# An FFT mixing layer before two MoE layers on one core: where the sums over thirds of x are made, in which step a weight decode takes its Abs, and by which order background sums are taken

## The chip, the cores and the metric

The kernel runs on one core of a Trainium2 chip. The metric is the time of one execution on the device in microseconds (us), taken as the median of several runs. The core has five engines with instruction queues of their own: TensorE (PE in the rows, PEld its weight loads), VectorE (DVE), ScalarE (ACT), GpSimd (POOL) and SyncE (SP, which here only issues transfers). Each queue is worked off in order; an instruction that waits holds everything behind it on its engine.

## The reference, cut to what matters

```python
def reference(x, w_r, w_i, b_r, b_i, moe.., moe2..):      # x: [4, 3072, 256] float32
    X = rfft(x, axis=1)                                    # per batch, along 3072
    Yr = Xr @ w_r - Xi @ w_i + b_r;  Yi = Xr @ w_i + Xi @ w_r + b_i
    Y = soft_threshold(Yr, 0.01) + 1j * soft_threshold(Yi, 0.01)
    y = irfft(Y, n=3072, axis=1)
    h = y @ w_in;  g = h * tanh(softplus(h));  z = g @ w_out      # moe, d_ff 2048
    # moe2: a token mix with the token before, relu(xk @ w_k)**2 @ w_v, times sigmoid(xr @ w_r)
```

The weights of the two MoE layers come as 64-bit floats and are decoded to 32 bits on the chip.

## The kernel before, in words

The program has two parts. `part1` (up to 361.54 us in the profiled execution) does the Fourier mixing of all four batches, one batch after the other; `part2` does the MoE layers and is laid out by a planner of its own (`Plan`). The change touches `part1` alone.

A sequence of 3072 is seen as 24 x 128. The forward transform takes radix sums over the 24 lines of x (`f1_ops`, VectorE, 128x1024 to 128x256 at a time) and then, for each of 12 residues, a product over the 128 (`emit_F`). A batch of x lies in SBUF as a tile `a` of 32 lines: three thirds of eight lines each (0 to 7, 8 to 15, 16 to 23, `load_third`), and eight lines (24 to 31) of room. There are two such tiles, in turn for the batches. The radix sums of a batch begin with the difference of the second and last third and with the sum of all three, called S here; then S - 3 times the first third, by `stt(..., -3.0, ...)` at L309, called the -3 combination here. S is made by transfers: after the difference, `sum_x` (L365) issues two accumulating transfers from GpSimd's queue, which add the second and the first third of x from DRAM onto lines 16 to 23. Batch 0 makes its sums by `f1_fast` and is not touched.

`part1` then runs a loop of 48 steps u (`NU`, twelve per batch, t = u % 12). TensorE's work of step u is the forward product F(u+1) (`emit_F`, or `emit_F3` with x split in a high and a low plane where u+1 is in `SPLIT_F`), the mixing product M(u) with the weights w_r and w_i (`emit_M`) and the inverse product I(u-1) (`emit_I`, split in planes where u-1 is in `SPLIT_I`). Behind them ScalarE and VectorE do: `post_F` (xh on ScalarE, xl on VectorE, both operands of M), `post_M` and `post_M2` (the threshold: yb on ScalarE, then on VectorE), for a split I the planes zh (ScalarE) and zl (VectorE), `post_I` (bs on ScalarE, then a store from SP to b_dr; bs has three buffers), and `preload` (the bias into a PSUM bank). The planes of the inverse matrices (imhi, imlo) come over GpSimd's queue into a ring of 12 slots (`load_stream`), a slot's next load being issued in the step that frees it.

Work off this path goes into the gaps of VectorE by `Background`: a queue `q` of the forward sums, each with a due step, and a list `f3` of the inverse radix sums of batch 0 (`f3_ops`, tile g, two jobs put in at steps 14 and 20, load of g first, stores to y_dr among the sums). `until(t)` issues such work while a clock that the program keeps by itself (70 ns + 1.04 ns an element) stays below t, always taking `q` first; `flush(due)` issues all of `q` that has come due; `drain` issues all that is left at step 42.

At steps 7 to 47 the weights of the first MoE layer are decoded by `Weights`: eight groups of w_in and four pieces of w_out. In step `first` of a piece ScalarE makes the sign (two instructions), VectorE builds the 32-bit word (two), and ScalarE takes Abs of it; in the step after, VectorE combines Abs with the sign and, for a group, makes four sums; later (`late`) ScalarE makes the high parts and VectorE, a step after that, the low parts. Groups 0 to 3 start at steps 11, 12, 23 and 24, groups 4 to 7 at 37 to 40, the pieces of w_out at 41 to 44; the high parts of the eight groups are at 35 to 42.

`new_a` (L694 on) loads all three thirds of batch b+2 from SP in step 10 of batch b, into a tile that it takes anew.

## Time and profile before

| | |
|---|---|
| median of 3 runs | 1910.03 us (1907.85 to 1910.5) |
| profiled execution | 1910.78 us, its span 1908.9 us |
| granted TensorE clock, mean | 0.989 |
| TensorE busy | 1856.1 us, 97% of the span |
| VectorE busy | 1427.9 us, 75% |
| ScalarE busy | 1220.8 us, 64% |
| GpSimd busy | 65.3 us, 3% |
| accumulating and other transfers on GpSimd's queue | 27.79 MB, 6.3% of 16 transfer engines |

The span is the stretch from the first to the last instruction. Times inside it are counted from its start. Loop step 6 begins at 54.65 us, step 12 at 106.27, step 24 at 185.73, step 32 at 245.62, step 40 at 299.03, step 46 at 348.73 (each the start of that step's F product); the second part begins at 361.54.

### The profile page before, as it was taken

To read this page: it belongs to the slowest core of one execution; us is meant where nothing else is said; L and a number is where in the kernel's file an instruction comes from. 1 tells how busy PE (TensorE), PEld (TensorE's weight loads), DVE (VectorE), ACT (ScalarE), POOL (GpSimd) and SP (SyncE) were. 2 spreads that over 40 slices of the span, in tenths; PEclk is the share of its full clock that TensorE was granted. 3 is DMA by queue.
4 is the path that set the end of the run, shared out by engine and by line. 5 is a ranking of instruction groups with operands and counts; after the bars stand their busy time and mean duration, and the time that the engine had idled before them with its cause. 6 is when DMAs were issued, how large, how long until landed. Compare 5 with 4: busy or idle time off the path is not lost.

```text
span 1908.9 us, 27281 instructions
## 1 busy us (share of the span) xinstructions
PE 1856.1 (97%) x9814; PEld 1602.4 (84%) x9814; DVE 1427.9 (75%) x2548; ACT 1220.8 (64%) x2194; POOL 65.3 (3%) x111
## 2 busy tenths in 40 slices
PE   9789897999999999999999999999999999999999
PEld 7678786788888888888888888888899999999998
DVE  8669797689888977778877777675676666667654
ACT  3245465667576575766757566574877777777775
POOL 1121221000000000000000000000000000000000
PEclk9899998999999999999999999999999999999999
DMA  9697979555566563646455554544422222222211
GB/s 314 133 246 209 229 201 289 195 174 167 152 202 190 159 190 117 190 132 192 153 174 160 161 188 140 163 152 130 139 83 67 67 67 67 67 67 69 70 51 34
DMA packets 192598, 283.87 MB, mean 149 GB/s; under 512 B 17104, under 2 KB 106960, under 8 KB 192208
## 3 DMA queue, kind: packets, MB, share of 16 engines
q1 hardware_dynamic: 173248, 253.29, 42.1%
q0 software_dynamic: 18144, 27.79, 6.3%
q8 instruction: 78, 1.28, 0.3%
q10 hardware_dynamic: 1072, 1.05, 0.2%
q14 instruction: 56, 0.46, 0.1%
HBM read 205.52 MB, written 76.55 MB: 148 GB/s over the span
## 4 chain that ended last, share of the span: by engine, by line
PE 88%; DMA 4%; DVE 4%; ACT 2%; SPq 1%; issue 1%; POOL 0%; ACTq 0%; DVEq 0%; POOLq 0%
PE a L218 27%; PE x L218 15%; PE v L218 14%; PE c L218 10%; PE z L218 5%; PE d L218 5%; PE zps L218 3%; PE yps L218 3%; DMA a<-in_x_dram 3%; PE xps L218 2%; PE bps L218 2%; DMA y_dr<-g 1%; DMA b_dr<-bs 1%; DVE g L209 1%; SPq L392 0%
## 5 line engine op out<-in xcount | busy, mean ns | idle before, releaser
L209 DVE TENSOR_TENSOR l<-k,h 128x512 fp32r<-128x512 f32 x576 | 391.6, 688 | 309.8 <-ACT h L215 155.0
L218 PE MATMUL a<-h,wo 128*128 128x512 f32 x1536 | 520.2, 389 | 0.0
L218 PEld LDWEIGHTS a<-h,wo 128*128 128x128 f32 x1536 | 288.3, 188 | 59.8
L218 PE MATMUL a<-l,wo 128*128 128x512 f32 x768 | 298.8, 389 | 0.0
L218 PE MATMUL v<-wv,h 128*128 128x256 f32 x1536 | 274.3, 278 | 0.0
L218 PEld LDWEIGHTS v<-wv,h 128*128 128x128 f32 x1536 | 244.3, 188 | 13.6
L218 PE MATMUL x<-yc,wr 128*128 128x512 f32 x864 | 243.5, 390 | 1.0 <-ACT c L215 1.0
L215 ACT ACTIVATE k<-c 128x512 f32<-128x512 f32 x288 | 172.7, 600 | 105.5 <-PE c L218 93.6
L215 ACT ACTIVATE c<-x 128x512 f32<-128x512 f32 x288 | 169.5, 589 | 92.4 <-PE x L218 77.9
L215 ACT ACTIVATE k<-k 128x512 f32<-128x512 f32 x288 | 178.2, 632 | 64.8 <-DVE k L209 62.3
L218 PE MATMUL v<-wv,l 128*128 128x256 f32 x768 | 213.0, 277 | 0.0
L218 PEld LDWEIGHTS x<-yc,wr 128*128 128x128 f32 x864 | 161.8, 188 | 36.2 <-ACT c L215 2.3
L215 ACT ACTIVATE d<-x 128x512 f32<-128x512 f32 x144 | 84.5, 587 | 147.9 <-PE x L218 146.6
L218 PEld LDWEIGHTS a<-l,wo 128*128 128x128 f32 x768 | 144.1, 188 | 30.3
L218 PE MATMUL c<-yc,wr 128*128 128x512 f32 x576 | 161.9, 389 | 0.0
L218 PEld LDWEIGHTS v<-wv,l 128*128 128x128 f32 x768 | 144.4, 188 | 0.0
L215 ACT ACTIVATE h<-k 128x512 fp32r<-128x512 f32 x192 | 118.7, 629 | 27.8 <-DVE k L212 25.8
L209 DVE TENSOR_TENSOR k<-d,zs 128x512 f32<-128x512 f32 x144 | 98.8, 686 | 44.7 <-PE d L218 44.6
L218 PEld LDWEIGHTS c<-yc,wr 128*128 128x128 f32 x576 | 108.1, 188 | 22.6
L209 DVE TENSOR_TENSOR yc<-src,yc 128x512 fp32r<-128x512 f32 x168 | 112.0, 686 | 14.4 <-ACT yc L215 14.0
L218 PE MATMUL x<-yc,wk 128*128 128x512 f32 x432 | 122.5, 392 | 0.0
L209 DVE TENSOR_TENSOR g<-g 128x128 f32<-128x128 f32 (+3 forms) x264 | 111.1, 443 | 0.9
(121 smaller groups left out, 2924.4 us busy)
## 6 DMA issues: line engine op xcount, KB each, us to landing
wr<-h_dr SPq DMA_DIRECT2D x288, 256.0 KB, 2.7
b_dr<-bs SPq DMA_DIRECT2D x48, 256.0 KB, 3.7
src<-y_dr SPq DMA_DIRECT2D x24, 512.0 KB, 4.3
wr<-h_dr SPq DMA_DIRECT2D x96, 128.0 KB, 2.1
xk_dr<-tm SPq DMA_DIRECT2D x48, 256.0 KB, 3.1
xr_dr<-tm SPq DMA_DIRECT2D x48, 256.0 KB, 3.1
src<-xk_dr SPq DMA_DIRECT2D x24, 512.0 KB, 4.3
xr<-xr_dr SPq DMA_DIRECT2D x24, 512.0 KB, 3.8
```

Of the source, the lines that this page charges most:

```text
L209: V.tensor_tensor(out=o, in0=a, in1=b, op=op)
L215: S.activation(out=o, in_=i, func=f, **kw)
L218: T.matmul(out=o, lhsT=l, rhs=r, start=start, stop=stop, **kw)
```

## The change

For batches 2 and 3 S is no longer made in lines 16 to 23 after the difference. In step 6 of the batch that uses the same tile before, SP loads the first third of x into lines 24 to 31 and the last third into 16 to 23, and `end_sum` adds the second and the last third onto 24 to 31 by accumulating transfers from GpSimd's queue, in halves; in step 10 SP loads the second and the first third. The tile is kept and not taken anew. For batch 1 S is made by VectorE, in four additions of 128x1024. The radix sums behind S use other lines in consequence, and a batch's forward sums all enter the queue in one step: step 4 for batch 1, step 0 of the batch ahead (12 and 24) for the others.

`until` takes inverse sums first while the next forward sum is due more than four steps ahead (`EARLY`).

Abs of a piece is issued in the step after its word, behind the high parts of that step on ScalarE, and the combination with the sign stands at the end of VectorE's work in that step. The high parts are issued right behind `post_M2`, and from step 35 on bs is copied behind xh. Steps 36 to 38 multiply F unsplit: `SPLIT_F` loses 37, 38 and 39.

```diff
@@ -35,14 +35,15 @@
 
 
 
-F1_AT = ((4, 6), (0, 3), (0, 3))
+F1_AT = ((4, 4), (0, 0), (0, 0))
+EARLY = 4
 START = (18600, 20500)
 SLACK = (2000, 3200)
 
 SUMS_AT = (11, 12, 23, 24)
 LOWS_AT = 35
 SPLIT_I = (*range(6, 10), *range(12, 22), *range(24, 34), *range(36, 47))
-SPLIT_F = (37, 38, 39, 44, 45, 46)
+SPLIT_F = (44, 45, 46)
 FIRST = tuple(u + 1 for u in SPLIT_I)
 F3_PART1 = {(1, 2): [(0, 0)], (1, 8): [(0, 1)]}
 ORD = [0, 1, 2, 3, 4, 6, 8, 10, 5, 7, 9, 11]
@@ -50,8 +51,8 @@
 F3_ORDER = [0, 1, 2, 3, 4, 5, 6, 7, 8, 9, 10, 14, 15, 11, 12, 13, 16, 17, 18, 19, 20, 27, 21, 22,
             23, 24, 25, 26, 30, 31, 28, 32, 29, 33, 34, 35, 41, 42, 36, 43, 37, 38, 44, 45, 39, 40, 46, 47]
 T_H, T_K = 10.22, 11.85
-LINES_G = [4, 5, 6, 7, 12, 13, 14, 15]
-LINES_F = [(20, 21), (22, 23), (18, 19), (16, 17),
+LINES_G = [4, 5, 6, 7, 12, 14, 13, 15]
+LINES_F = [(20, 22), (21, 23), (18, 19), (16, 17),
            (24, 25), (2, 10), (28, 29), (3, 11), (26, 27), (6, 14), (30, 31), (7, 15)]
 
 
@@ -305,18 +306,20 @@
         l1 = lambda l: A[:, l]
         one = lambda n, f: [(n, f)]
         head = [
+            halves(8, lambda i, j: tt(L(24 + i, 24 + j), L(8 + i, 8 + j), L(16 + i, 16 + j), ADD)),
             halves(8, lambda i, j: tt(L(8 + i, 8 + j), L(16 + i, 16 + j), L(8 + i, 8 + j), SUB)),
-            halves(8, lambda i, j: stt(L(i, j), L(i, j), -3.0, L(16 + i, 16 + j), MULT, ADD)),
-            one(4, lambda: tt(L(24, 28), L(16, 20), L(20, 24), ADD)),
-            one(4, lambda: tt(L(28, 32), L(16, 20), L(20, 24), SUB)),
-            one(2, lambda: tt(L(16, 18), L(24, 26), L(26, 28), ADD)),
-            one(2, lambda: tt(L(18, 20), L(24, 26), L(26, 28), SUB)),
-            one(1, lambda: tt(l1(20), l1(16), l1(17), ADD)),
-            one(1, lambda: tt(l1(21), l1(16), l1(17), SUB)),
-            one(1, lambda: tt(l1(16), l1(29), l1(31), SUB)),
-            one(1, lambda: tt(l1(17), l1(29), l1(31), ADD)),
-            one(2, lambda: stt(L(22, 24), L(16, 18), HALF, L(28, 31, 2), MULT, ADD)),
-            one(2, lambda: stt(L(16, 18), L(16, 18), -HALF, L(28, 31, 2), MULT, ADD)),
+            halves(8, lambda i, j: tt(L(24 + i, 24 + j), L(i, j), L(24 + i, 24 + j), ADD)),
+            halves(8, lambda i, j: stt(L(i, j), L(i, j), -3.0, L(24 + i, 24 + j), MULT, ADD)),
+            one(4, lambda: tt(L(16, 20), L(24, 28), L(28, 32), ADD)),
+            one(4, lambda: tt(L(20, 24), L(24, 28), L(28, 32), SUB)),
+            one(2, lambda: tt(L(24, 26), L(16, 18), L(18, 20), ADD)),
+            one(2, lambda: tt(L(18, 20), L(16, 18), L(18, 20), SUB)),
+            one(1, lambda: tt(l1(16), l1(21), l1(23), SUB)),
+            one(1, lambda: tt(l1(17), l1(21), l1(23), ADD)),
+            one(2, lambda: stt(L(21, 24, 2), L(16, 18), HALF, L(20, 23, 2), MULT, ADD)),
+            one(2, lambda: stt(L(16, 18), L(16, 18), -HALF, L(20, 23, 2), MULT, ADD)),
+            one(1, lambda: tt(l1(20), l1(24), l1(25), ADD)),
+            one(1, lambda: tt(l1(22), l1(24), l1(25), SUB)),
         ]
         rows = lambda f: [(4, lambda r=r: f(r)) for r in range(2)]
         tail = [
@@ -362,9 +365,11 @@
             for a in (1, 2, 0):
                 load_third(A, b, a, 8 * a, nc.scalar if b == 0 and a == 2 else nc.sync, lo, up)
 
-    def sum_x(A, b):
-        for a in (1, 0):
-            load_third(A, b, a, 16, nc.gpsimd, accum_op=ADD)
+    def end_sum(A, b):
+        for lo in (0, 4):
+            load_third(A, b, 1, 24, nc.gpsimd, lo, lo + 4, accum_op=ADD)
+        for lo in (0, 4):
+            load_third(A, b, 2, 24, nc.gpsimd, lo, lo + 4, accum_op=ADD)
 
     def f3_ops(b, h):
         st = {}
@@ -466,7 +471,8 @@
         def add(self, ops, due=0):
             self.q.extend((c, e, due) for c, e in ops)
 
-        def step(self):
+        def step(self, u=0):
+            self.u = u
             if self.wait:
                 self.wait -= 1
             if not self.f3 and self.jobs:
@@ -486,7 +492,9 @@
         def until(self, t):
 
             while True:
-                q = self.q or (self.f3 if not self.wait else None)
+                q = self.q
+                if self.f3 and not self.wait and (not q or q[0][2] > self.u + EARLY):
+                    q = self.f3
                 if not q or self.clock + q[0][0] > t:
                     return
                 o = q.pop(0)
@@ -630,13 +638,13 @@
         def put(self, step, make, first, late):
             def load():
                 p = make()
-                for u, k, f in ((first, 0, lambda: p[1]()), (first + 1, 0, lambda: p[2]()), (late + 1, 0, lambda: p[4]()),
-                                (first, 1, lambda: p[0]()), (late, 1, lambda: p[3]()), (first, 2, lambda: p[5]())):
+                for u, k, f in ((first, 0, lambda: p[1]()), (first + 1, 4, lambda: p[2]()), (late + 1, 0, lambda: p[4]()),
+                                (late, 1, lambda: p[3]()), (first + 1, 2, lambda: p[5]()), (first, 2, lambda: p[0]())):
                     self.at.setdefault((u, k), []).append(f)
             self.at.setdefault((step, 3), []).append(load)
 
-        def vec(self, u):
-            return [op for f in self.at.get((u, 0), []) for op in f()]
+        def vec(self, u, k=0):
+            return [op for f in self.at.get((u, k), []) for op in f()]
 
         def sca(self, u, k):
             return [op for f in self.at.get((u, k), []) for op in f()]
@@ -926,14 +934,14 @@
             for u in range(NU):
                 b, t = divmod(u, NT)
                 if b + 1 < NB:
-                    if t == F1_AT[b][0]:
-                        head, tail = f1_ops(As[b + 1])
-                        bg.add(priced(head[:1]) + [(0.0, lambda b=b: sum_x(As[b + 1], b + 1))], NT * (b + 1))
-                    if t == F1_AT[b][1]:
-                        for ops, due in ((head[1:], 0), (tail[:10], 4), (tail[10:], 8)):
-                            bg.add(priced(ops), NT * (b + 1) + due)
+                    for k in range(2):
+                        if t == F1_AT[b][k]:
+                            head, tail = f1_ops(As[b + 1])
+                            early = head[1:2] if b else head[:2]
+                            for ops, due in ((head[2 + (b > 0):], 0), (tail[:10], 4), (tail[10:], 8)) if k else ((early, 0),):
+                                bg.add(priced(ops), NT * (b + 1) + due)
                 bg.jobs += F3_PART1.get((b, t), [])
-                bg.step()
+                bg.step(u)
                 if u == SUMS_AT[0] - 4:
                     wf = src_p.tile([128, 4, 8, 128], F32, tag="src", name="wsrc")
 
@@ -961,9 +969,9 @@
                 if u:
                     bg.until(y_at + (900 if u - 1 in SPLIT_I else SLACK[0]))
                     post_M2(u - 1)
-                    if u in FIRST:
-                        if u >= SUMS_AT[0] - 3:
-                            emit(wq.sca(u, 1))
+                    if u >= SUMS_AT[0] - 3:
+                        emit(wq.sca(u, 1))
+                    if u in FIRST and u < LOWS_AT:
                         post_I(u - 2)
                     y_at = bg.spend(y_at, 602)
                     if u - 1 in SPLIT_I:
@@ -971,21 +979,23 @@
                         bg.until(y_at + 900)
                         split_lo(u - 1)
                         y_at = bg.spend(y_at + 900, 602)
+                if u >= SUMS_AT[0] - 3:
+                    emit(wq.sca(u, 2))
                 if u + 1 < NU:
                     bg.until(pe + 700 + SLACK[1] * (u > 0))
                     post_F(u + 1)
                     x_next = bg.spend(pe + 700, 602)
                 if u >= SUMS_AT[0] - 3:
-                    if u not in FIRST:
-                        emit(wq.sca(u, 1))
                     bg.flush(-1)
-                    emit(wq.sca(u, 2))
+                    for c, e in wq.vec(u, 4):
+                        bg.clock += c
+                        e()
                     emit(wq.load(u))
                 if u + 2 in SPLIT_F:
                     split_x(u + 2, 0)
                     split_x(u + 2, 1)
                     bg.clock += 602
-                if u > 1 and u not in FIRST:
+                if u > 1 and (u not in FIRST or u >= LOWS_AT):
                     post_I(u - 2)
                 emit_M(u, None if u else 1)
                 if u + 2 < NU:
@@ -1002,8 +1012,14 @@
                     load_fwd(u + NT)
                 if u == 1:
                     P.tensor_copy(out=zero[:, 32:33], in_=xt[2][0][:, 0, 0:1].bitcast(F32))
+                if t == NT - 6 and b + 2 < NB:
+                    A = As[b + 2] = As[b]
+                    load_third(A, b + 2, 0, 24, nc.sync)
+                    end_sum(A, b + 2)
+                    load_third(A, b + 2, 2, 16, nc.sync)
                 if t == NT - 2 and b + 2 < NB:
-                    new_a(b + 2)
+                    for a in (1, 0):
+                        load_third(As[b + 2], b + 2, a, 8 * a, nc.sync)
                 while sent < len(stream) and (sent < RING and u or sent >= RING and stream[sent - RING][0] <= u):
                     load_stream(sent)
                     sent += 1
```

## Rows read from the trace of the kernel before

**Rows 1.** Busy time by stretch: PE, PEld, DVE, ACT, POOL, clock, DMA share, GB/s.
```profile
54.65:106.27 51.62, 37.61 (x185) 32.18 (x184) 35.41 (x54) 18.00 (x32) 9.05 (x13) 0.87 0.72 170
106.27:138.78 32.51, 25.56 (x138) 22.63 (x136) 17.53 (x28) 14.45 (x28) 8.51 (x10) 0.90 0.97 248
138.78:185.73 46.95, 46.95 (x253) 41.17 (x253) 44.35 (x82) 24.13 (x44) 7.42 (x14) 1.00 0.67 188
185.73:245.62 59.89, 53.15 (x265) 45.88 (x264) 47.08 (x79) 24.29 (x45) 13.34 (x19) 0.91 0.87 226
245.62:299.03 53.41, 48.50 (x275) 42.88 (x274) 45.04 (x97) 32.53 (x62) 10.70 (x20) 0.97 0.81 240
299.03:348.73 49.70, 38.68 (x205) 32.97 (x205) 37.30 (x70) 32.72 (x65) 5.28 (x10) 0.93 0.82 261
361.54:1908.90 1547.36, 1542.43 (x8206) 1330.66 (x8204) 1146.58 (x2060) 1046.93 (x1865) 4.37 (x11) 1.00 0.42 130
```

**Rows 2.** Timeline of TensorE, starts of F products: start, length, what, [idle before].
```profile
42.27 1.89 PE L218 MATMUL xps<-fm,a 128*128 128x256 f32 x8
...
48.46 1.89 PE L218 MATMUL xps<-fm,a 128*128 128x256 f32 x8
...
100.89 1.06 PE L218 MATMUL xps<-fm,a 128*128 128x128 f32 x8
...
106.27 1.89 PE L218 MATMUL xps<-fm,a 128*128 128x256 f32 x8
...
112.60 1.89 PE L218 MATMUL xps<-fm,a 128*128 128x256 f32 x8
...
118.53 1.89 PE L218 MATMUL xps<-fm,a 128*128 128x256 f32 x8
...
282.98 0.70 PE L218 MATMUL xps<-fmhi,yc 128*128 128x256 f32 x4
...
288.76 1.46 PE L218 MATMUL xps<-fm,a 128*128 128x256 f32 x6
```

**Rows 3.** Timelines of TensorE and VectorE, stalls of the loop.
```profile
67.60 1.23 DVE L212 SCALAR_TENSOR_TENSOR a<-a 128x1024 f32<-128x1024 f32 x1 [14.23 <-issue]
...
73.27 3.78 PE L218 MATMUL bps<-im,yb 128*128 128x256 f32 x8 [14.01 <-DVE yb L212]
...
130.06 1.22 DVE L212 SCALAR_TENSOR_TENSOR a<-a 128x1024 f32<-128x1024 f32 x1 [8.29 <-DMA a<-in_x_dram]
...
136.06 1.22 PE L218 MATMUL bps<-imhi,zh 128*128 128x256 f32 x4 [6.95 <-ACT zh L215]
...
217.43 2.07 PE L218 MATMUL yps<-wmh,xl 128*128 128x512 f32 x4 [3.27 <-DVE xl L209]
...
313.77 0.73 PE L218 MATMUL bps<-imhi,zh 128*128 128x256 f32 x4 [2.55 <-ACT zh L215]
```

**Rows 4.** GpSimd's timeline; landing times of SP's loads of x, and of planes.
```profile
53.08 2.71 POOL L356 DMA_DIRECT2D a<-in_x_dram x2 [16.00 <-DVE a L209]
...
60.83 2.66 POOL L356 DMA_DIRECT2D a<-in_x_dram x2 [5.04 <-DMA a<-in_x_dram]
...
DMA to landing us min/median/max: 5.1/9.1/14.0
...
imhi<-in_sel_dram POOLq DMA_DIRECT2D x35, 256.0 KB, 5.4
```

**Rows 5.** Timeline of ScalarE near step 30.
```profile
234.19 0.60 ACT L215 ACTIVATE bs<-bps 128x512 f32<-128x512 f32 x1 [7.48 <-DMA b_dr<-bs]
```

**Rows 6.** Groups of ScalarE and VectorE, 54.65:361.54: busy, mean ns, idle before.
```profile
L215 ACT ACTIVATE wsrc<-wsrc 128x512 f32<-128x512 f32 x8 | 5.0, 624 | 13.2 <-DVE wsrc L212 13.2
...
L215 ACT ACTIVATE q<-q 128x512 f32<-128x512 f32 x4 | 2.5, 630 | 10.2 <-DVE q L212 10.2
...
L209 DVE TENSOR_TENSOR a<-a 128x1024 f32<-128x1024 f32 x28 | 33.2, 1219 | 0.1
...
L209 DVE TENSOR_TENSOR zl<-yb,zh 128x512 fp32r<-128x512 f32 x35 | 24.2, 692 | 28.2 <-ACT zh L215 27.3
```

## The prediction

> **What bounds the kernel now.** I read three views in turn. First the stretches [rows 1]: in the last one, from 361.54 us to the end, TensorE is busy 1542.43 of 1547.36 us at a granted clock of 1.00. The change touches nothing there, so that stretch can only move as a block. All that can be won lies in the 361.54 us ahead of it. There TensorE stands in every stretch but one (138.78 to 185.73).
>
> Second, what a loop step takes when nothing disturbs it, from the starts of neighbouring F products [rows 2]. With the inverse product unsplit (steps 3 to 6): 48.46 - 42.27 = 6.19 us. With it split: 118.53 - 112.60 = 5.93. The short step ahead of a new batch: 106.27 - 100.89 = 5.38, the first of a batch: 112.60 - 106.27 = 6.33. With a split F ahead: 288.76 - 282.98 = 5.78. The stretches of rows 1 against the sum of such steps:
>
> - steps 6 to 11: 51.62 - (6.19 + 4 x 5.93 + 5.38 = 35.29) = 16.33
> - 12 to 15: 32.51 - (6.33 + 3 x 5.93 = 24.12) = 8.39
> - 16 to 23: 46.95 - (7 x 5.93 + 5.38 = 46.89) = 0.06
> - 24 to 31: 59.89 - (6.33 + 7 x 5.93 = 47.84) = 12.05
> - 32 to 39: 53.41 - (4 x 5.93 + 5.38 + 6.33 + 2 x 5.78 = 46.99) = 6.42
> - 40 to 45: 49.70 - (3 x 5.93 + 3 x 5.78 = 35.13) = 14.57
>
> Together 57.82 us are lost in steps 6 to 45; these steps need 294.08 - 57.82 = 236.26 us. The loss counts the idle time and what follows it: the eight products behind the 14.01 us stall take 3.78 us where they take 1.89 elsewhere [rows 2, 3], the stretch's clock being 0.87 [rows 1].
>
> Third, what each stall waits for. At 73.27, 136.06 and 217.43 TensorE waits for a yb, zh or xl [rows 3]; each of these stands on VectorE or just behind it, and VectorE itself stands 14.23 and 8.29 us in front of the -3 combination of the forward sums [rows 3], which reads the lines that the accumulating transfers fill. These are started only once VectorE has made the first difference: GpSimd waits 16.00 us for it, the second transfer goes out 60.83 - 53.08 = 7.75 us after the first, and the combination starts 6.8 us later [rows 3, 4]. That is the loss of steps 6 to 31, 36.8 us, save what the 7.48 us of ScalarE behind the stores of bs cost near step 30 [rows 5]. In steps 36 to 45 the stalls are 1 to 3 us each, such as 2.55 us for a zh [rows 3]. There ScalarE waits 13.2 and 10.2 us for the decode's words [rows 6], because Abs is queued in the step in which VectorE builds the word, and everything behind it on ScalarE (preload, yb, high parts, zh) waits too.
>
> **The change part by part.**
>
> **Accumulating transfers.** For the second batch (batch 1) they vanish: four additions of 128x1024 take their place, 4 x 1.219 = 4.88 us of VectorE [rows 6], and no transfer stands in the middle of its sums. For the third and fourth (2 and 3) the copy of x goes out in step 6 of the batch two earlier, and the two accumulating ones follow it on GpSimd's queue. A copy lands in 5.1 to 14.0 us [rows 4], an accumulating leg takes 7.75 to 9.4 (60.83 to the second half of the combination at 70.26, one op and 1.43 us behind 67.60) [rows 3, 4]. From 59 us at the end of step 6 that is 59 + 9.1 + 7.75 + 9.4 = 85 us, at worst 59 + 14.0 + 2 x 9.4 = 92. VectorE wants the result only behind the second batch's sums: these are some 30 us (twelve ops of 1024 and more in the head, the rest smaller), and a step leaves some 3.5 us beside its three fixed ops of 0.69, so it is step 14, at 102 us on the new time scale. Cover of 10 to 17 us; the fourth batch has more, as two jobs of inverse sums now go ahead of its head. So 36.8 us go, save the half microsecond of step 24, where ScalarE waits for xl to make the copies of a batch's first block; I leave 0.5.
>
> What it moves past: SP issues four transfers in step 6 and four in step 10 in place of six in step 10, with one store of bs a step behind them: three buffers of bs are cover for three steps; without it the price is that of the third rival. On GpSimd the planes of the inverse product queue behind the accumulating transfers, some 18 to 25 us from the wait for the copy to the last issue. A plane is fetched six steps ahead (12 slots, two a step), 35.6 us, and lands in 5.4 [rows 4]: 30 us of cover.
>
> A page speaks against this part: the Trainium skill's "SBUF — State Buffer", section on its two separate sides ("A DMA issued from the GpSimd (POOL) queue is SWDGE"), says that VectorE in a two-port mode keeps GpSimd from writing the descriptors of its transfers, so that they seem blocked. Until now the accumulating transfers ran while VectorE stood; now they run beside it. By that rule the time would be that of the last rival below. This trace speaks against it: from 138.78 to 185.73 VectorE is busy 44.35 of 46.95 us, GpSimd issues transfers of planes all the while, and TensorE, which reads them, never stands [rows 1].
>
> **Abs one step later.** ScalarE's 23.4 us of waiting for words go [rows 6]; the word is then a step old. The added wait is VectorE's combination with the sign, which now stands at the end of the step behind xl; Abs is ahead of xh on ScalarE, so it is done when xl is. ScalarE is busy 32.72 us in steps 40 to 45 [rows 1], 5.45 a step against 5.86 needed: full, but under. It now follows as it can, and I leave 0.5 us a step in the four steps with a whole group each, 2.0 us. Cost bounds: 0, and 7 (half of the 14.57 lost there now).
>
> **Fewer split F.** Three steps lose a ScalarE and a VectorE op (-3 x 0.69 = -2.06 us there) and TensorE needs 5.93 instead of 5.78 in two of them: +0.30 us.
>
> **Order of sums by due step.** It moves work and adds none: inverse sums go while the forward ones are not due. What decides is whether VectorE fits at all. Its busy time in steps 6 to 45 is 35.41 + 17.53 + 44.35 + 47.08 + 45.04 + 37.30 = 226.71 us [rows 1]; + 4.88 - 2.06 = 229.53, against 236.56 us of TensorE: 97%. The one stretch without a loss held 44.35/46.95 = 94.5%. At that share VectorE needs 243.0 us, so 6.4 us remain as stalls, somewhere near steps 36 to 43, where decode and sums meet. Its bounds: 0 (VectorE fills all), and 29.1: every zl waits 0.8 us for zh (28.2 us / 35 [rows 6]), 13.6% of a step, and at a share of 86.4% it needs 265.7 us. I take 6.4, the share measured where both engines were full.
>
> **Sum.** 57.82 - 0.30 - 0.5 - 2.0 - 6.4 = 48.6 us. The profiled execution took 1910.78 us (span 1908.9 and 1.9 around it): 1910.78 - 48.6 = 1862.2. It lies 0.75 us above the median of 1910.03, less than the sum can tell. Predicted 1862.
>
> **The rivals.**
>
> **VectorE paces the whole part.** With the upper bound above: 57.8 - 0.3 - 2.5 - 29.1 = 25.9 us, 1884.9. For it: 97% leaves no room, and the planner fills the gap ahead of zl with at most 900 ns of work, so no 1024 op fits. Against it: steps 16 to 23 ran at 94.5% with such ops.
>
> **The late steps keep their loss.** The wait only moves, from Abs on ScalarE to the sign on VectorE, and ScalarE's 5.45 us a step stays the limit: 6.42 + 14.57 remain in place of the 8.9 that I leave, 12.1 us more, 1874. Against it: ScalarE's waits there are as long as the stalls and all have that one source.
>
> **The transfers are not early.** If the loads into lines 24 to 31 wait for all readers of the tile, they stand until step 10 on SP, with the stores of bs behind them: three buffers of bs last three steps, and some 7 us a batch are lost (7.48 in rows 5 is such a wait), twice: 1876. For it: it is the same tile, not a new one. Against it: nothing in these lines is read after step 6.
>
> **Slower: GpSimd's queue starves the inverse product.** A hold over 30 us makes the planes late, and each further microsecond is lost in both batches; slower than before from 30 + 48.6/2 = 54 us of hold. At 60 us it would be 1910.8 - 48.6 + 60 = 1922. The legs would have to be three times as long as those of rows 4. The rule of the Trainium skill weighed above would be a way to that; no run here shows it.
>
> **How the numbers follow.** Forecast 0.68 (its own range 1854 to 1872: no remainder at all gives 1910.8 - 57.5 = 1853.3, and 10 us more than I leave gives 1872); VectorE 0.13; late steps 0.10; not early 0.05; starved planes 0.03; no difference (gains and holds cancel) 0.01. 0.2% is 3.8 us, about what the runs of this kernel can tell. Faster 0.68 + 0.13 + 0.10 + 0.05 = 0.96, same 0.01, slower 0.03. The range runs from 1854 to 1880: it holds the forecast, the late steps, the transfers that are not early and half of the VectorE case.
>
> **What would show it.** Right: no VectorE wait for a transfer of x in steps 5 to 35; steps 6, 15, 28 and 30 near 5.9 us; ScalarE no longer waiting for the decode's words; the last stretch as long as now, starting near 313 us; VectorE's share ahead of it near 94%. Wrong: TensorE waiting for planes (starved), ScalarE waiting for stores of bs near steps 8 to 11 and 20 to 23 (not early), zh and xl late by a little in every step (VectorE), steps 38 to 45 still over 7 us (late steps). The forecast fails most likely by the 6.4 us: if sums come due in a lump, the loss there is larger.

## The result and the profile after

The changed kernel takes 1867.26 us (median of 4 runs, 1866.11 to 1868.55) against 1909.58 (4 runs), a ratio of 0.978 with a 95% interval of 0.9763 to 0.9797. The forecast was 1862.0, in a range of 1854 to 1880. The profiled execution took 1867.44 us, its span 1865.7, so the two spans differ by 43.2 us.

The same stretches of loop steps as in [rows 1], cut at the starts of the F products of steps 6, 12, 16, 24, 32, 40 and 46, then the second part (columns: start:end, length, busy time of PE, PEld, DVE, ACT, POOL with instructions, granted clock, DMA share, GB/s):

```profile
54.41:89.66 35.25, 35.25 (x185) 30.77 (x184) 32.81 (x49) 18.68 (x33) 12.54 (x16) 1.00 1.04 265
89.66:115.97 26.31, 24.88 (x138) 21.41 (x137) 22.92 (x39) 13.56 (x26) 3.18 (x6) 1.00 0.78 245
115.97:162.84 46.87, 46.87 (x255) 41.08 (x253) 44.39 (x83) 23.64 (x43) 14.21 (x20) 1.00 0.94 238
162.84:218.95 56.11, 50.43 (x265) 44.32 (x264) 47.30 (x98) 25.00 (x46) 6.84 (x13) 0.94 0.75 227
218.95:266.65 47.70, 47.53 (x262) 41.71 (x261) 44.99 (x76) 29.86 (x57) 9.02 (x17) 1.00 0.82 240
266.65:304.32 37.67, 35.63 (x206) 31.00 (x205) 35.24 (x67) 34.17 (x68) 4.88 (x10) 1.00 0.96 326
316.71:1865.70 1548.99, 1543.23 (x8210) 1331.68 (x8208) 1147.33 (x2062) 1047.73 (x1865) 4.38 (x11) 1.00 0.42 130
```

Against the sums of undisturbed steps that the prediction used (35.29, 24.12, 46.89, 47.84, 47.29 with three F products unsplit, 35.13), the loss is now 0, 2.19, 0, 8.27, 0.41 and 2.54 us: 13.4 in place of 57.8.

The second part needs like marks. The changed kernel's 316.71 is its first product with the weights wr; the 361.54 us at which the second part of the kernel before was said to begin is the second group of such products. The first one there, on TensorE's timeline, and the stretch from it (as in the rows above):

```profile
360.64 1.05 PE L218 MATMUL x<-yc,wr 128*128 128x512 f32 x3
```

```profile
360.64:1908.90 1548.26, 1543.33 (x8210) 1331.40 (x8208) 1147.26 (x2062) 1047.44 (x1865) 4.37 (x11) 1.00 0.42 130
```

Both stretches now hold the same 8210 products, and the second part takes 0.7 us longer (1548.99 against 1548.26). Steps 46 and 47 take 0.5 us longer (12.39 against 11.91), and step 6 begins 0.2 us earlier. Steps 6 to 45 take 249.91 us in place of 294.08, 44.2 less: 44.2 + 0.2 - 0.5 - 0.7 = 43.2, the difference of the spans.

In steps 6 to 11 TensorE now never stands, where it stood 14.01 us [rows 3]. More than half of what is left is one place. The stalls of TensorE in steps 24 to 31 come down to this one on its timeline (start, length, what, [idle before <- what ended it]):

```profile
179.50 1.22 PE L219 MATMUL bps<-imhi,zh 128*128 128x256 f32 x4 [5.68 <-ACT zh L216]
```

The zh that it waits for stands on ScalarE behind a copy into bs; ScalarE's timeline:

```profile
178.33 0.60 ACT L216 ACTIVATE bs<-bps 128x512 f32<-128x512 f32 x1 [8.04 <-DMA b_dr<-bs]
178.82 0.62 ACT L216 ACTIVATE zh<-yb 128x512 fp32r<-128x512 f32 x1
```

That copy needs one of the three buffers of bs, and the store that would free it had not been issued. SP's own queue (SPq; the length is from the first to the last of the xN transfers):

```profile
151.78 8.92 SPq L397 DMA_DIRECT2D y_dr<-g  x9
170.49 0.32 SPq L382 DMA_DIRECT2D g<-b_dr  x1
170.86 0.43 SPq L861 DMA_DIRECT2D b_dr<-bs  x1
171.33 5.08 SPq L359 DMA_DIRECT2D a<-in_x_dram  x4
176.45 3.63 SPq L861 DMA_DIRECT2D b_dr<-bs  x3
```

The reader is to see the hole from 160.7 to 170.49. The first job of inverse sums has stored its results from tile g; the load of the second job writes the same tile and waits until those stores have landed (the view of SP's waits gives `g<-b_dr` one wait of 9.5 us for `y_dr<-g`). Everything behind it on SP, four loads of x and four stores of bs, waits with it though it needs neither. The load is that of the job put in the list at step 20, and it falls in step 25.

That the stores land late can be seen from the transfers issued from 140 to 175 us (DMA: busy tenths of the transfer engines in 40 slices; then what was issued, count, KB each, median us from issue to landing):

```profile
DMA  9999999979999999999999999999999310069999
imhi<-in_sel_dram POOLq DMA_DIRECT2D x6, 256.0 KB, 10.4
y_dr<-g SPq DMA_DIRECT2D x10, 64.0 KB, 9.5
a<-in_x_dram POOLq DMA_DIRECT2D x1, 512.0 KB, 9.8
```

The transfer engines are full up to 167 us (31 slices of 0.875 us, all but one of them at nine tenths or more). The accumulating transfers of batch 3 (the tile a on GpSimd's queue) and the planes of the inverse product that were held behind them share them with the stores. The last accumulating transfer, issued at 150.80 us, lands 9.8 us later, at 160.6, when the last of the stores is being issued; so what these last stores meet are the planes and the stores ahead of them. The gap in the row, from 167 to 171 us, is the end of SP's wait: little is under way, and nothing new is issued until the last store has landed, at 170.2.

### The profile page after: what moved, and what is told of

Read it like the earlier page. It is cut to its first block, busy times and chain, and to the rows that moved or that the text cites. A ratio compares the mean times of both kernels' runs of the same rounds, so it can differ in the third digit from the quotient of the medians.

```text
span 1865.7 us, 27256 instructions
## 1 busy us (share of the span) xinstructions
PE 1847.0 (99%) x9802; PEld 1595.6 (86%) x9802; DVE 1430.6 (77%) x2549; ACT 1219.7 (65%) x2191; POOL 60.1 (3%) x105
## 3 DMA queue, kind: packets, MB, share of 16 engines
q0 software_dynamic: 15232, 24.12, 5.2%
## 4 chain that ended last, share of the span: by engine, by line
PE 85%; DVE 9%; DMA 3%; ACT 2%; issue 1%; SPq 0%; ACTq 0%; POOL 0%
PE a L219 28%; PE x L219 16%; PE v L219 14%; PE c L219 10%; PE z L219 5%; PE d L219 5%; PE zps L219 4%; DVE a L210 3%; DVE a L213 1%; PE yps L219 1%; DVE yb L213 1%; DMA y_dr<-g 1%; DVE xl L210 1%; PE bps L219 1%; ACT zh L216 1%
## 5 line engine op out<-in xcount | busy, mean ns | idle before, releaser
L216 ACT ACTIVATE k<-c 128x512 f32<-128x512 f32 x288 | 172.7, 600 | 106.2 <-PE c L219 94.3
```

The lines of the kernel that those rows point to most:

```text
L216: S.activation(out=o, in_=i, func=f, **kw)
```

## The experiments

Lengths of the stretches in us, by steps, each from the starts of F products (the before of the table ran with the changed kernel; each experiment's ratio is against runs of before beside it, whose medians are 1908.24 to 1909.21; the last stretch ends at the first product with wr):

| kernel | 6-11 | 12-15 | 16-23 | 24-31 | 32-39 | 40-45 | 46-47 | median us | ratio (95%) |
|---|---|---|---|---|---|---|---|---|---|
| before | 51.62 | 32.51 | 46.95 | 59.89 | 53.41 | 49.70 | 11.91 | 1909.58 | |
| changed | 35.25 | 26.31 | 46.87 | 56.11 | 47.70 | 37.67 | 12.39 | 1867.26 | 0.9763 to 0.9797 |
| job2_later | 35.26 | 26.27 | 46.88 | 49.42 | 48.67 | 37.65 | 12.42 | 1860.64 | 0.9734 to 0.9763 |
| no_acc3 | 35.25 | 26.08 | 46.88 | 49.44 | 48.58 | 37.68 | 12.41 | 1861.86 | 0.9740 to 0.9769 |
| q_first | 35.24 | 26.29 | 46.87 | 49.31 | 52.21 | 49.41 | 12.38 | 1875.34 | 0.9807 to 0.9840 |
| abs_back | 35.25 | 24.76 | 47.53 | 53.72 | 53.08 | 47.04 | 11.91 | 1879.30 | 0.9833 to 0.9862 |
| sums_back | 52.30 | 32.27 | 47.56 | 49.92 | 63.15 | 36.75 | 12.87 | 1899.37 | 0.9935 to 0.9968 |
| abs_alone | 51.80 | 33.51 | 48.53 | 55.52 | 50.54 | 38.64 | 13.39 | 1893.92 | 0.9907 to 0.9936 |
| sums_alone | 35.25 | 24.61 | 47.42 | 48.88 | 50.98 | 61.54 | 11.91 | 1886.48 | 0.9865 to 0.9898 |
| splitf_back | 35.25 | 26.08 | 46.87 | 56.35 | 48.32 | 41.77 | 11.91 | 1872.15 | 0.9791 to 0.9820 |
| job2_room | 35.25 | 25.02 | 47.28 | 48.57 | 48.58 | 38.63 | 12.40 | 1861.42 | 0.9736 to 0.9765 |
| job2_split2 | 35.26 | 26.30 | 46.87 | 49.47 | 48.18 | 37.10 | 12.90 | 1861.43 | 0.9735 to 0.9765 |
| job2_nosplit | 35.25 | 26.29 | 46.87 | 49.46 | 48.18 | 36.65 | 12.61 | 1859.80 | 0.9728 to 0.9757 |

What lies ahead of step 6 takes 54.1 to 56.0 us in these thirteen profiles: 54.4 in the changed kernel, and 55.5 to 56.0 in four kernels that do not differ from it there. Where two totals differ by less than 2 us, the stretches say more than the totals.

### The stall of step 25: queue order or late landing

The second job of inverse sums is put in the list at step 26 in place of step 20:

```diff
-F3_PART1 = {(1, 2): [(0, 0)], (1, 8): [(0, 1)]}
+F3_PART1 = {(1, 2): [(0, 0)], (2, 2): [(0, 1)]}
```

> The second job of inverse sums (its load of g and its sums) is put in at step 26 in place of step 20; all else as in the changed kernel. Theory (SP's queue): in the changed kernel SP stands 9.5 us on the load of g until the last stores to y_dr have landed, the stores of bs stand behind it, and ScalarE's 8.04 us for a free bs make the one large stall left (5.68 us, 8.3 us with what follows). With the load issued after they have landed, that wait is gone, steps 24 to 31 take 47.8 us in place of 56.1, and the time is 1867.3 - 8.3 = 1859. Rival (VectorE paces, 97% of TensorE's time): the same sums in fewer steps only move the loss to steps 36 to 43: 1865 to 1869. Third: the engines of the transfers are full there whatever SP waits for, and the stall comes with the loads of x: 1865 or more, with the wait on another store.

Measured: 1860.64 us; steps 24 to 31 take 49.42 us, 6.7 less. SP's queue near the same place:

```profile
164.80 0.37 SPq L861 DMA_DIRECT2D b_dr<-bs  x1
165.73 4.29 SPq L359 DMA_DIRECT2D a<-in_x_dram  x4
170.12 2.33 SPq L861 DMA_DIRECT2D b_dr<-bs  x3
172.51 0.95 SPq L382 DMA_DIRECT2D g<-b_dr  x1
```

The loads of x and the stores of bs now go out ahead of the load of g, and ScalarE's wait for a buffer of bs ahead of that zh shrinks from 8.04 to 0.70 us:

```profile
170.77 0.60 ACT L216 ACTIVATE bs<-bps 128x512 f32<-128x512 f32 x1 [0.70 <-DMA b_dr<-bs]
```

The stores of y_dr still land late here (median 7.5 us), so late landing alone costs little: it needs something queued behind it. Of the 49.42 us, 1.6 are left over the undisturbed 47.84, nearly all of them in step 25 (7.54 us): its yb stands on VectorE behind the combination with the sign and four sums.

The other theory's experiment leaves the queue as it is and takes the accumulating transfers of batch 3 away; its sum then holds the first third of x alone:

```diff
-                    end_sum(A, b + 2)
+                    if b == 0:
+                        end_sum(A, b + 2)
```

> Leaves out the accumulating transfers of batch 3 (its sum over thirds then holds the first third alone); all else as in the changed kernel. Theory (the stores of y_dr land late because the accumulating transfers and the planes held back by them fill the transfer engines): the last stores, issued at 160.7 us, land in about 4 us and not in 10, SP's wait on the load of g falls from 9.5 to 3 or 4 us, ScalarE's wait for bs from 8.0 to about 2, time about 1861. Rival (SP's order alone, the landing is slow without them too): the wait for bs stays within 1 us of 8.0 and the time at 1866 to 1868.

Measured: 1861.86 us, steps 24 to 31 at 49.44. ScalarE has no wait for bs there any more, and the load of g goes out at 160.64:

```profile
151.72 5.80 SPq L397 DMA_DIRECT2D y_dr<-g  x9
160.64 0.32 SPq L382 DMA_DIRECT2D g<-b_dr  x1
```

The time from issue to landing of the stores of y_dr issued from 140 to 200 us, first in the changed kernel, then in this one:

```profile
DMA to landing us min/median/max: 5.5/8.8/11.2
```

```profile
DMA to landing us min/median/max: 2.7/3.5/5.8
```

So the stall needs both the order on SP's queue and the late landing, and the landing is late through the accumulating transfers and what they hold back: with either taken away, steps 24 to 31 are 6.7 us shorter. Which of the two delays the stores, the accumulating transfers or the planes that then come in a bunch, is not separated. Busy transfer engines alone do not: from 140 to 175 us they are at nine tenths or more in 30 of 40 slices of this run too (34 in the changed kernel), and move 285 GB/s on the mean where the changed kernel moves 259.

### The order of sums

Forward sums always go first, as before the change:

```diff
-EARLY = 4
+EARLY = 10 ** 6
```

> Forward sums always ahead of inverse ones (the order of the kernel before); all else as in the changed kernel. Theory (VectorE has no room, so order matters): the second inverse job is not through by step 38, its rest is drained in a lump at step 42 as in the kernel before (4.4 us of g operations in steps 42 and 43), and steps 40 to 45 lose 4 to 6 us more than the 2.5 of the changed kernel; the wait of SP on the load of g moves to a later step and costs between 0 and 8 us there. Time 1866 to 1873, middle 1871. Rival (the order is worth nothing once no transfer stands in the middle): 1867 within 1.

Measured: 1875.34 us, 8.1 more than the changed kernel and above the range expected. Steps 24 to 31 became shorter by 6.8 us, because the load of g moved away from the busy place; steps 32 to 45 became longer by 16.3, of which 10.16 us are one wait of TensorE, at 298.79 us. VectorE's timeline ahead of it:

```profile
284.99 2.17 DVE L210 TENSOR_TENSOR g<-g 128x256 f32<-128x256 f32 x9
...
293.71 3.69 DVE L213 SCALAR_TENSOR_TENSOR g<-g 128x512 f32<-128x512 f32 x6
...
297.33 0.68 DVE L213 SCALAR_TENSOR_TENSOR yb<-yps,yb 128x512 f32<-128x512 f32 x1
```

These are inverse sums that were not done by step 42 and are drained there in one lump, and the next step's yb stands behind them. The order by due step earns most of its worth by keeping this lump from forming: 16.3 us in the late steps, of which it gives back 6.8 by the stall of step 25. job2_later keeps all but 1.0 us of the one (86.3 against 85.4 in steps 32 to 45) and does not pay the other.

### Abs alone, and all but Abs

In the changed kernel, Abs, the high parts, the combination with the sign and the copy into bs go back to their old places:

```diff
-                for u, k, f in ((first, 0, lambda: p[1]()), (first + 1, 4, lambda: p[2]()), (late + 1, 0, lambda: p[4]()),
-                                (late, 1, lambda: p[3]()), (first + 1, 2, lambda: p[5]()), (first, 2, lambda: p[0]())):
+                for u, k, f in ((first, 0, lambda: p[1]()), (first + 1, 0, lambda: p[2]()), (late + 1, 0, lambda: p[4]()),
+                                (first, 1, lambda: p[0]()), (late, 1, lambda: p[3]()), (first, 2, lambda: p[5]())):
...
-                    if u in FIRST and u < LOWS_AT:
+                    if u in FIRST:
+                        if u >= SUMS_AT[0] - 3:
+                            emit(wq.sca(u, 1))
                         post_I(u - 2)
```

> Abs again in the step of its word, with the places of the high parts, of the sign's combination and of bs of the kernel before; all else as in the changed kernel. Theory (ScalarE standing on the word is what the late steps lost): ScalarE's waits for the word, 23.4 us in the kernel before and 0 in the changed one, come back, steps 40 to 45 take about 47 us in place of 37.7 and steps 36 to 39 some 4 us more: 1867.3 + 13 = 1880. Rival (the late loss came from the lump of inverse sums and the split of F): steps 40 to 45 stay under 40 us and the time under 1871.

Measured: 1879.30 us, 12.0 more. ScalarE's groups for the two kinds of words, in this kernel (busy, mean ns | idle before):

```profile
L216 ACT ACTIVATE wsrc<-wsrc 128x512 f32<-128x512 f32 x8 | 5.0, 627 | 13.0 <-DVE wsrc L213 13.0
L216 ACT ACTIVATE q<-q 128x512 f32<-128x512 f32 x4 | 2.5, 630 | 9.1 <-DVE q L213 9.1
```

and in the changed kernel:

```profile
L216 ACT ACTIVATE wsrc<-wsrc 128x512 f32<-128x512 f32 x8 | 4.9, 618 | 0.0
L216 ACT ACTIVATE q<-q 128x512 f32<-128x512 f32 x4 | 2.5, 616 | 0.0
```

The waits of [rows 6] come and go with the place of Abs, and the time with them: steps 32 to 45 are 14.8 us longer with the waits. Steps 12 to 15 are 1.55 us shorter; that is the price of the combination with the sign in steps 12 to 14, told below. The four places were moved together in this run and the next, so what each is worth alone is not shown.

The kernel before, with those four places alone changed (the same lines the other way round):

> The kernel before with Abs, the sign's combination, the high parts and bs in the changed places, and nothing else of the change. Theory: ScalarE's waits for the word go (23.4 us), steps 32 to 45 lose 21.0 us now; the inverse sums' lump and the split F of steps 36 to 38 stay, so about half of that is gained: 1909 - 11 = 1898, within 4. Rival (Abs alone does it all): 1909 - 18 = 1891. Third (Abs is worth nothing without room on VectorE): 1905 or more.

Measured: 1893.92 us, 15.3 less than before, between the two expectations (11 and 18 us of gain). Steps 40 to 45 go from 49.70 to 38.64.

### The sums and transfers alone, and all but these

In the changed kernel, the sums over thirds of x, their transfers, their lines and their start steps go back; the rest stays:

```diff
-F1_AT = ((4, 4), (0, 0), (0, 0))
+F1_AT = ((4, 6), (0, 3), (0, 3))
...
-    def end_sum(A, b):
-        for lo in (0, 4):
-            load_third(A, b, 1, 24, nc.gpsimd, lo, lo + 4, accum_op=ADD)
-        for lo in (0, 4):
-            load_third(A, b, 2, 24, nc.gpsimd, lo, lo + 4, accum_op=ADD)
+    def sum_x(A, b):
+        for a in (1, 0):
+            load_third(A, b, a, 16, nc.gpsimd, accum_op=ADD)
...
                 if t == NT - 2 and b + 2 < NB:
-                    for a in (1, 0):
-                        load_third(As[b + 2], b + 2, a, 8 * a, nc.sync)
+                    new_a(b + 2)
```

> The sums over thirds as in the kernel before (difference first, then the accumulating transfers onto lines 16 to 23, all loads in step 10, the old steps of the forward sums); Abs, due-step order and three split F as in the changed kernel. Theory (two thirds of the gain is the transfers out of the middle of the sums): VectorE's waits for x near steps 6, 15 and 28 come back, 14, 8 and 2 to 5 us, and steps 6 to 31 lose 30 to 37 us; the late steps keep their gain of 18: 1909 - 18 = 1891, or 1886 to 1896. Rival (inverse sums by due step would have filled the wait): VectorE works on inverse sums while the transfers run, steps 12 to 31 lose under 10 us, 1880 or less.

Measured: 1899.37 us, 32.1 more than the changed kernel and 8 above the expectation. Two stalls of the kernel before are back as expected, 13.73 us in step 6 (waiting for yb) and 6.68 in step 15, each behind a VectorE that waits for a transfer of x; the one near step 28 is not:

```profile
72.82 3.78 PE L219 MATMUL bps<-im,yb 128*128 128x256 f32 x8 [13.73 <-DVE yb L213]
```

The excess is a stall that was not expected, at step 32, which makes steps 32 to 39 15.4 us longer than in the changed kernel (TensorE, then VectorE, on their timelines):

```profile
252.84 2.07 PE L219 MATMUL yps<-wmh,xl 128*128 128x512 f32 x4 [12.58 <-DVE xl L210]
```

```profile
250.96 1.23 DVE L213 SCALAR_TENSOR_TENSOR a<-a 128x1024 f32<-128x1024 f32 x1 [15.80 <-issue]
252.10 0.68 DVE L210 TENSOR_TENSOR xl<-xps,xh 128x512 fp32r<-128x512 f32 x1
```

VectorE stood 15.80 us in front of the -3 combination of batch 3 with xl queued behind it. With inverse sums taken first, the chain of difference, transfers and -3 combination starts later for this batch (GpSimd issues its first transfer at 236.10 us, in the kernel before at 194.74), and lands where xl needs the engine. The kernel abs_alone, told above, differs from this one by the order and the three split F alone: it has no such stall, and its steps 32 to 39 take 50.54 us. So the order by due step is good only together with sums that wait for no transfer.

The kernel before, with this part alone changed (Abs, order and split F as before):

```diff
-F1_AT = ((4, 6), (0, 3), (0, 3))
+F1_AT = ((4, 4), (0, 0), (0, 0))
+EARLY = 10 ** 6
...
-                    if t == F1_AT[b][0]:
...
+                    for k in range(2):
+                        if t == F1_AT[b][k]:
...
+                if t == NT - 6 and b + 2 < NB:
+                    A = As[b + 2] = As[b]
+                    load_third(A, b + 2, 0, 24, nc.sync)
+                    end_sum(A, b + 2)
+                    load_third(A, b + 2, 2, 16, nc.sync)
...
```

> The kernel before with the sums over thirds and their loads as changed, and nothing else of the change. Theory (the parts add: Abs costs 12 us when put back, the order 8, the split F 5): 1867.3 + 25 = 1892, so 17 us gained alone of the 36.8 that steps 6 to 31 lose, as VectorE's saved time comes back as a lump of inverse sums near step 42. Rival (the transfers' stalls go whatever the rest does): steps 6 to 31 lose under 5 us and steps 32 to 45 as much as before, 21: 1909 - 32 = 1877. Third (late steps lose more than before, since what was done during the stalls is now missing): above 1892.

Measured: 1886.48 us, 21.8 less than before, between the two expectations. Steps 6 to 31 take 156.2 us in place of 191.0 and stand 2 us above the undisturbed ones, so 34.8 of the 36.8 us of early loss are gone; but steps 40 to 45 go from 49.70 to 61.54, with a stall of 8.99 us in step 43. Ahead of that stall VectorE works on g from 292.78 to 305.4 us, the same lump as in q_first. VectorE's idle time was not only lost time: sums pushed out of the gaps come due later, beside the decode.

### Split F

The three steps that the change took out of the list are put back:

```diff
-SPLIT_F = (44, 45, 46)
+SPLIT_F = (37, 38, 39, 44, 45, 46)
```

> F of steps 37 to 39 split again; all else as in the changed kernel. Theory (a split F saves TensorE 0.15 us a step and costs a ScalarE and a VectorE op of 0.6 and 0.69 us where both are full): steps 35 to 38 lose 2 to 4 us for yc as in the kernel before (1.34 and 0.69 us), 1867.3 + 2.5 = 1870. Rival (TensorE's time counts): 1867.3 - 0.3 = 1867.0.

Measured: 1872.15 us, 4.9 more. The size was expected, the place was not: steps 32 to 39 take 0.6 us more, steps 40 to 45 4.1 more. In the profiled execution steps 6 to 47 take 4.2 us more in all, and what lies ahead of step 6 takes 1.3 more. The two instructions a step displace sums, and these are late four steps on. VectorE's timeline at the start of step 43 shows it:

```profile
287.95 0.68 DVE L210 TENSOR_TENSOR yc<-a,yc 128x512 fp32r<-128x512 f32 x1
288.56 2.81 DVE L213 SCALAR_TENSOR_TENSOR a<-a 128x256 f32<-128x256 f32 x3
```

The last three sums of batch 3 stand behind the split of F(44), which reads lines 2 and 10 of tile a, and these are among the lines that the three write; in the changed kernel the last of them starts at 279.12 us, ahead of that split. So this kernel's F(44) takes x before its sums are done and its output is another one; the instructions are those of the split, and the run is read for their time only.

### Versions from job2_later

Three versions build on the step-26 kernel. One leaves room on VectorE in steps with a combination with the sign, so that the background work in front of it is less by 1550 ns of the program's own clock:

```diff
-                    bg.until(pe + 700 + SLACK[1] * (u > 0))
+                    bg.until(pe + 700 + SLACK[1] * (u > 0) - (1550 if u > 7 and (u, 4) in wq.at else 0))
```

> The changed kernel with the second inverse job at step 26, and with 1.55 us less of background work ahead of xl in the steps in which the sign's combination and the four sums follow xl. Theory (the stalls left at steps 13, 14, 25, 39 and 41, 1.05 + 0.34 + 1.36 + 0.80 + 0.79 us of idle time, are yb late by that work, which the program's clock does not see ahead of time): these go, and with what follows them 4 to 6 us: 1860.6 - 5 = 1856. Rival (VectorE is full, work put off comes due later): the loss moves to steps 40 to 45, 1859 to 1862.

Measured: 1861.42 us, no better than 1860.64. The early stalls shrink as meant (12 to 15 by 1.25 us, 24 to 31 by 0.85), and steps 40 to 45 grow by 1.0: part of the work put off comes due later, as the rival had it. Steps 6 to 47 are 0.8 us shorter in all, and the profiled execution spends 1.8 us more ahead of step 6, so the total does not show it.

The others take more split F products away, `SPLIT_F = ()` and `SPLIT_F = (45, 46)`:

> The second inverse job at step 26, and no F split at all (steps 43 to 45 now unsplit too); all else as in the changed kernel. Theory (steps 43 and 44 still lose 1 to 2 us, as TensorE waits 1.06 us for yc, made by ScalarE and VectorE where both are full): these losses go, TensorE needs 0.15 us more in three steps, 1860.6 - 1 = 1859.5. Rival (the split pays for itself): 1861 or more.

> The second inverse job at step 26, and F split in steps 44 and 45 alone; all else as in the changed kernel. Theory: only the first split F comes late (1.06 us of idle time and what follows in step 43); without it 1860.6 - 1.3 = 1859.3. Rival: the next one comes late in its place, 1860.6 within 0.5.

Measured: 1859.80 and 1861.43 us. The first is the fastest kernel of this study, 7.5 us under the changed one; its interval (0.9728 to 0.9757) overlaps that of job2_later, so of the 7.5 us only the step of the second job is shown to matter. Its stretches of steps 32 and 40 on:

```profile
212.15:260.33 48.18, 47.53 (x263) 41.71 (x261) 46.73 (x85) 29.68 (x57) 7.42 (x14) 1.00 0.82 244
260.33:296.98 36.65, 35.86 (x195) 30.97 (x194) 32.96 (x64) 32.48 (x65) 3.28 (x7) 1.00 0.93 318
```

Without split F, VectorE has 32.96 us of work in the last stretch in place of 35.24, and ScalarE 32.48 in place of 34.17.

## Why the prediction was right, and by what it was off

**The mechanism.** The sums over thirds and Abs did what the prediction said; the order by due step and the split F did something else besides, told below. Kernels that undo a part lose 32.1 (sums and transfers), 12.0 (Abs), 8.1 (order) and 4.9 us (split F). These add up to 57.1, not to the 42.3 of the change, and the two parts that were done alone, the sums and Abs, gain 21.8 and 15.3: each part's gain rests on the others. The sum over stretches was the safer way to the total, since it asked how much loss could remain and not what each edit is worth.

**"So 36.8 us go, save the half microsecond of step 24", and "It moves work and adds none".** Here the prediction was off most. Steps 6 to 31 kept 2.19 + 8.27 = 10.5 us, not 0.5. The first reason is a wait for bs like that of [rows 5], which the prediction counted among what goes. SP's queue of the kernel before tells where that one came from:

```profile
204.26 10.09 SPq L392 DMA_DIRECT2D y_dr<-g  x11
223.32 0.32 SPq L377 DMA_DIRECT2D g<-b_dr  x1
223.69 1.47 SPq L853 DMA_DIRECT2D b_dr<-bs  x3
```

The same hole, 214 to 223, the same load of g at its end, three stores of bs behind it. The new sums and transfers do take this wait away, as the term had it: in sums_alone and q_first, which have them in the old order, the load of g goes out at 231.03 and 234.84 us, ScalarE never waits for a store of bs, and steps 24 to 31 take 48.88 and 49.31 us; in abs_alone, with the old transfers, the wait is there (6.8 us). So the 36.8 were sized nearly right (34.8 in sums_alone), and the step that failed is the one on the order of sums, "It moves work and adds none". It moved the stores and the load of g too, to 144 to 170 us, beside the accumulating transfers that the change had put at 137 to 161 us for batch 3. The wait came back 5 steps earlier and cost 8.3 us with the 1.6 that the sign and its sums take in the same step. The prediction named three buffers of bs as cover for three steps, but asked only whether x would use it up, and did not ask what else the new order would put on SP's queue.

The second reason is the 2.19 us that steps 12 to 15 keep, nearly all in 12 to 14, whose decode the prediction had not priced: its 2.0 us for "the four steps with a whole group each" were worked out from steps 40 to 45. VectorE's timeline in step 13:

```profile
98.34 0.68 DVE L210 TENSOR_TENSOR xl<-xps,xh 128x512 fp32r<-128x512 f32 x1
98.94 0.68 DVE L213 SCALAR_TENSOR_TENSOR wsrc<-wsrc,sg 128x512 f32<-128x512 f32 x1
99.65 1.02 DVE L210 TENSOR_TENSOR wsrc<-wsrc 128x128 f32<-128x128 f32 x4
100.59 0.68 DVE L213 SCALAR_TENSOR_TENSOR yb<-yps,yb 128x512 f32<-128x512 f32 x1
```

The combination and its four sums, 1.65 us, now stand between xl and yb. In abs_back and sums_alone, where they stand elsewhere, steps 12 to 15 take 24.76 and 24.61 us in place of 26.31: some 1.6 of the 2.19 us are theirs. Where the other 0.6 comes from is not shown.

**"6.4 us remain as stalls, somewhere near steps 36 to 43", and 2.0 for ScalarE.** Steps 32 to 45 keep 0.41 + 2.54 = 2.95 us where 6.4 + 2.0 were left. The share that the 6.4 came from, 94.5%, looks well met: VectorE is busy 44.99 of 47.70 us (94.3%) and 35.24 of 37.67 (93.5%), and 44.39 of 46.87 (94.7%) where nothing is lost. Over steps 6 to 45, without the 8.27 us of the stall, it is 227.65 us (the sum of the six stretches) in 249.91 - 8.27 = 241.64, 94.2%. But it is no limit: in job2_nosplit VectorE is busy 46.73 of 48.18 us in steps 32 to 39, 97.0%, and these lose 0.9 us against 47.29. The place was not met either: of 13.4 - 8.27 = 5.1 us that remain beside the stall, 2.2 lie in steps 12 to 15. So no run shows the 94.2% over all to be more than a coincidence, and the two terms together were too large by 5.4 us. VectorE had 227.65 us to do, 1.9 less than was counted. ScalarE waits 4.6 us in all for the sums ahead of the high parts (yc), a wait that the prediction did not have. Behind one such wait, 1.53 us at 282.23, TensorE waits 0.8 us for a zh and 1.1 us for the first split F; how much of that it causes is not shown.

**+0.30 us for the split F.** TensorE does take that much more, but it is not what the edit is worth: the unsplit products win 4.9 us, through VectorE's work four steps later. The prediction had this only as 2.06 us less to do, and spread it over all steps.

**The second part "can only move as a block".** By like marks it became 0.7 us longer. It has one new wait of TensorE, 1.2 us for a load of weights (columns: engine and what waits <- for what: us in all, times, longest):

```profile
PE z L219 <- DMA wr<-h_dr: 1.2, 1, 1.2
```

Of the other twelve profiles two have it (0.4 and 1.9 us, in job2_room and job2_split2). Why the load is late there was not tried.

Counted together: 9.96 us more than was left in steps 6 to 31, 5.45 less in steps 32 to 45, 0.48 more in steps 46 and 47, 0.69 more in the second part and 0.24 less ahead of step 6: 5.44 us, near the 5.2 by which the profiled 1867.44 lies above 1862.2. That the total came this near is in part luck, as the two large misses have opposite signs.

**The tests named beforehand.** Steps 6, 15, 28 and 30 take 6.19, 5.93, 5.92 and 5.93 us. VectorE has no wait for a transfer of x in steps 5 to 35. The second part starts at 316.71, or at 317.60 by the mark that the prediction used, not near 313; the stall of step 25 is more than the difference. The cover for the accumulating transfers was sized right: GpSimd holds from 55.4 to 77.7 us, 22 us in a forecast of 18 to 25, and no plane came late:

```profile
62.98 3.86 POOL L359 DMA_DIRECT2D a<-in_x_dram  x3 [7.58 <-DMA a<-in_x_dram]
71.79 2.17 POOL L359 DMA_DIRECT2D a<-in_x_dram  x2 [4.95 <-DMA a<-in_x_dram]
76.37 1.28 POOL L359 DMA_DIRECT2D a<-in_x_dram  x1 [2.42 <-issue]
```

**The rivals.** VectorE pacing the whole part fell: two stretches at 94% of VectorE lose 0 and 0.4 us, and one at 97% in job2_nosplit 0.9. The late steps did not keep their loss (20.99 to 2.95). Transfers that are not early: they were early (SP issues the first ones at 58.0 to 60.1 us, in step 6); the wait for bs that this rival would have shown did appear, by another way and at another step, and about at the price of one such wait (8.3 against 7.5 or so). Starved planes: none came late, though VectorE was busy 32.81 of 35.25 us while GpSimd issued. The rule that the Trainium skill's "SBUF — State Buffer" gives in its section "SBUF: two separate sides", that VectorE in a two-port mode keeps GpSimd from writing descriptors, is not tested by this: no run here shows that an instruction that VectorE ran is in such a mode. So what the prediction held against the rule, a busy VectorE beside GpSimd's transfers, does not speak against it either; it shows that these instructions did not starve the transfers. The accumulating ones landed as follows, first in the kernel before, in part beside a VectorE that stood, then in the changed one, beside a VectorE at 93 to 95%:

```profile
DMA to landing us min/median/max: 6.7/7.9/13.0
DMA to landing us min/median/max: 6.7/8.5/10.9
```

## What to carry to other kernels

A wait for a buffer is a question to the queue that frees it: list what that queue has in front of the freeing transfer, and above all a load that waits for stores to land, for it holds everything behind it that needs neither. When work is put in another order, ask which loads and stores move with it and what they will meet there: that an order adds no work does not mean that it adds no wait. When a stall is taken away, price each remaining wait by its own cause and not by the stretch it stands in; and ask of idle time that goes what work had used the gaps, since part of a gain can come back as a lump at the next due step. Undoing one part at a time showed 57 us in a change of 42: parts that share an engine's free time are worth less or more alone than together, so test the pair too.

## What the runs showed of the hardware that was not expected

What one queue issues can slow the stores of another: stores of 64 to 192 KB from SP landed in a median of 3.5 us without batch 3's accumulating transfers on GpSimd's queue, and in 8.8 us with them and the planes held behind them. From 140 to 175 us the transfer engines were at nine tenths or more in 30 of 40 slices without them and in 34 with them, but moved 285 GB/s on the mean without and 259 with them. The stall of TensorE that came of it stood two engines and two queues away.

Accumulating transfers of 128 to 768 KB took about as long to land beside a VectorE at 93 to 95% (median 8.5 us) as in the kernel before, where VectorE stood for part of that time (median 7.9).
